# An MLP behind attention on one core: GpSimd rounds the sums of weights, the second bias is loaded first, and the steps of the norm and of the operands stand further apart

## The chip, the cores and the metric

The kernel runs on one core of a Trainium2 chip. A core has TensorE (PE, matrix products, fed by weight loads, PEld), VectorE (DVE), ScalarE (ACT), GpSimd (POOL) and SyncE (SP), which here issues the DMAs. Each engine works through its own instructions in order; they wait for one another by semaphores. The metric is device time in microseconds (us).

## What is computed

One transformer block over 2048 tokens of width 576: modulated layer norm, attention with 32 query heads and one key and value head, and then the part that the change touches, a second modulated norm and an MLP of width 4608.

```python
mod = (_silu(c) @ w_mod).reshape(c.shape[0], 6, 1, -1)
sa, ca, ga, sb, cb, gb = (mod[:, 0], mod[:, 1], mod[:, 2], mod[:, 3], mod[:, 4], mod[:, 5])
h = _layernorm(x, axis=-1) * (1 + ca) + sa
x = x + ga * _A_ref(h, A_wq, A_wk, A_wv, A_wo)          # attention
h = _layernorm(x, axis=-1) * (1 + cb) + sb
x = x + gb * _B_ref(h, B_w1, B_b1, B_w2, B_b2)
# inside _B_ref:
y = _layernorm(x, axis=-1)
h = _gelu(jnp.einsum("bsd,df->bsf", y, w1) + b1)
return jnp.einsum("bsf,fd->bsd", h, w2) + b2
```

## The kernel before

All matrix products are made at close to float32 accuracy from rounded parts. An operand is split in a high part (rounded to `F32R`) and a low part (what the rounding left), and a product is the sum of three: high by high, high by low, low by high. So each operand takes a copy that rounds ("hi") and a subtraction ("lo").

The MLP stage runs over halves of the tokens (1024 each, two blocks of 512) and, within a half, over 18 groups of 256 hidden columns: 36 rounds (`for v in range(NV)`). The product with `w1` of a round covers two blocks of tokens and two halves of the columns, a 2 by 2 by 2 matrix product in blocks, and is made in Strassen's way, with seven products of sums instead of eight. So both operands are needed as sums:

- The weights. `load_w1` brings the raw group into one buffer (`w1r`) a round ahead. `w1_sum(a)` makes the sums numbered 4, 6, 10 and 12 in a scratch tile (`w1s`) on GpSimd and then rounds each with `w1_hi` on ScalarE (L652, into `w1a`); `w1_sum_lo` takes the low part on GpSimd (L655). `w1_a`, `w1_22` and `w1_tails` do the same for the parts that are no sums. This is spread over the round before the one that uses them.
- The tokens. `op_pieces` makes the seven operands (`ops`, and `opt` for the last 64 rows) of a half from the normed tokens `yr`: "+X" rounds piece X on ScalarE (L880), "-X" takes its low part (L882), "=X" forms the difference on VectorE (L873). For the first half they are made at the end of the attention stage and in round 0; for the second half in round 17.

A round goes through its seven products (`product`, L934, into the PSUM tiles `psB`), adds them up on VectorE, runs four `gelu` generators (each alternates between ScalarE and VectorE, and ends with a high part on ScalarE, L953, and a low part on GpSimd, L954), and between them takes the eight tiles of the product with `w2` of the round before (`t_()`, generator `fc2`, L969, into the two tiles `psA`; VectorE adds each into the residual `XT`, L973). The order on each engine is the order of this code. `g_()` steps each gelu once.

Seven calls of `more()` a round place other work. In rounds 1 to 9 they step the second norm of the second half (`ln2_block(2)`, `ln2_block(3)`, four tiles of 128 tokens each): statistics (L138 and the lines after on VectorE, L144 and L145 on GpSimd), apply (L533 on VectorE, L535 and L536 on GpSimd), statistics again, apply again (L547), add the bias `b2` to the residual (L551 on GpSimd), and transpose with PE (L150, evacuated by ScalarE L160 and VectorE L162). A tile takes seven steps, so one a round. The first step also loads the bias `b2g` and scales it on GpSimd (L562 to L564).

PSUM has two `psA` and four `psB` tiles here; a new `psB` must wait until the one that it takes over has been read.

Of the kernel before, what the change touches and what calls it, by code (L numbers as in the profile page):

```python
# [18 lines left out]
KD = 5  # L19
# [13 lines left out]
def block_kernel(ctx: ExitStack, tc, x, wqkv, wo, w1, b1, w2, b2, c, wmod, ident_in, out):  # L33
# [19 lines left out]
    def psB(): return PS["t"].tile([128, 512], F32, name="psB", bufs=PS["b"])  # L53
# [463 lines left out]
    def ln2_tile(tb, t):  # L517

        X = XT[:, NT * tb + t, :]

        def small():
            return (per.tile([128, 2], F32, name="mv2", bufs=2), per.tile([128, 1], F32, name="rs2", bufs=2))

        fine = tb < 2
        mv, rs = small()
        stt = ln_stats1(X)
        if fine:
            yield
# [4 lines left out]
        (po if fine else ve).tensor_scalar(h, X, mv[:, 0:1], rs, op0=ALU.subtract, op1=ALU.mult)  # L533
        e = po if fine else ve
        po.tensor_mul(h, h, BC[:, 1, :])  # L535
# [10 lines left out]
        e = po if fine else ve  # L546
        e.tensor_scalar(h, h, mv[:, 0:1], rs, op0=ALU.subtract, op1=ALU.mult)  # L547
        e.tensor_copy(Z[:, D:], Z[:, 512:D])
        if fine:
            yield  # L550
        po.tensor_tensor(X, X, B2["b"], op=ALU.add)  # L551
        yield
        yr = YR[tb // 2][:, KD * (tb % 2):KD * (tb % 2 + 1)]
        transpose_tile(Z, yr, t, 0, 4, ac)
        yield
        transpose_tile(Z, yr, t, 4, 5, ve)
        yield

    def ln2_block(tb):
        if "b" not in B2:  # L560
            b2g = B2["b"] = px.tile([128, D], F32, name="b2g")
            sy.dma_start(b2g, b2.to_broadcast([128, D]))  # L562
            po.tensor_mul(b2g, b2g, BC[:, 2, :])
            po.tensor_scalar(b2g, b2g, 2.0, None, op0=ALU.mult)  # L564
# [68 lines left out]
    W1 = {}  # L633
# [4 lines left out]
    def w1_rooms():  # L638
        while prep:
            step(prep)  # L640
        W1["a"] = px.tile([128, KD, 2, 128], F32, name="w1r")
        t = px.tile([128, 3, 128], F32, name="w1s")
        W1["s"], W1["d"] = t[:, :2], t[:, 2]

    def w1_raw(f, h):
        return W1["a"][:, 2 * h:2 * h + 2, f, :]

    def load_w1(i):
        sy.dma_start(W1["a"].rearrange("p k f c -> p k (f c)"), w1[i])

    def w1_hi(a, n, src):
        ac.activation(W1["r"][:, a:a + n], src, AF.Copy)  # L652
# [4 lines left out]
    def w1_a(e=po):  # L657
        src = W1["a"][:, :KD - 1, 0, :]
        w1_hi(0, 4, src)
        w1_lo(0, 4, src, e)  # L660

    def w1_22(e=po):
        w1_hi(8, 2, w1_raw(1, 1))
        w1_lo(8, 2, w1_raw(1, 1), e)

    SUMS = {4: "S2", 6: "S3", 10: "S1", 12: "S4"}

    def w1_sum(a, e=po):

        o = W1["s"]  # L670
        def op(x, y, how):
            e.tensor_tensor(o, x, y, op=how)  # L672
        if SUMS[a] == "S3":
            op(w1_raw(0, 0), w1_raw(1, 0), ALU.subtract)
        elif SUMS[a] == "S4":
            op(w1_raw(0, 1), W1["r"][:, 4:6].bitcast(F32), ALU.subtract)
            op(o, W1["r"][:, 21:23].bitcast(F32), ALU.subtract)
        else:
            op(w1_raw(1, 0), w1_raw(1, 1), ALU.add)
            if SUMS[a] == "S2":  # L680
                op(o, w1_raw(0, 0), ALU.subtract)
        w1_hi(a, 2, o)

    def w1_sum_lo(a, e=po):
        w1_lo(a, 2, W1["s"], e)

    def w1_tails(e=po):

        t, d = W1["a"][:, KD - 1], W1["d"]
        ac.activation(W1["r"][:, 14:16], t, AF.Copy)  # L690
# [24 lines left out]
    def first_split():  # L715
        w1_tile()
        w1_rooms()
        load_w1(0)
        for _ in range(3):
            yield  # L720
        w1_sum(4, ve)
        w1_a()
        w1_sum_lo(4, ve)
        yield
        w1_sum(6, ve)
        w1_22()
        w1_sum_lo(6, ve)
        yield
        w1_sum(10, ve)
        w1_sum_lo(10, ve)  # L730
        yield
        w1_sum(12, ve)
        w1_sum_lo(12, ve)
        yield
        w1_tails()
        yield


# [177 lines left out]
    W2 = W2[:2], W2[2:]  # L916
    B2.clear()
    NV = 2 * NG

    def load_w2(v):  # L920
# [61 lines left out]
    def t_():  # L982
        next(f2, None)

    def g_():

        for gen in list(gens):
            if next(gen, 0) == 0:
                gens.remove(gen)

    for v in range(NV):
        nx = v + 1 < NV
        if v == NG - 1:
# [12 lines left out]
        load_w2(v)  # L1006
        ba = psB()
        product(ba, 0, 0)
        ac.activation(U[:, 0], ba, AF.Copy)
# [12 lines left out]
        if nx:  # L1022
            w1_sum(4)
        more("-T2 =T3", "-T1 -t1")
        t_()
        if v == 1:
            t_()
        if nx:
            w1_sum_lo(4)
        product(ba, 2, 2, False, (0, 0))  # L1030
        gens.append(gelu(v, 0, 0, ba))
        g_()
        if nx:
            w1_a()
            w1_sum(6)
        more("+T3 +B21 -B21", "-T4")
        t_()
        if nx:
# [9 lines left out]
        if nx:  # L1048
            w1_sum(10)
        more("-T3 =T4 =T1 +T1", "-B22")  # L1050
        t_()
        if nx:
            w1_sum_lo(10)
        g_()
        product(bc, 8, 12, False, (1, 0))
        ve.tensor_tensor(bc, bc, U[:, 0], op=ALU.add)
        g_()
        gens.append(gelu(v, 1, 0, bc))
        g_()
        if nx:  # L1060
            w1_22()
        more("-T1 +T4 +t0 -t0")
        t_()
        g_()
        t_()
        product(bd, 12, 4, False, (2, 1))
        ve.tensor_tensor(bd, bd, U[:, 0], op=ALU.add)
        g_()
        gens.append(gelu(v, 0, 1, bd))
        g_()  # L1070
        t_()
        if nx:
            w1_sum(12)
            w1_tails()
            w1_sum_lo(12)
# [48 lines left out]
```

## Time and profile before

| | us |
|---|---|
| median of 3 runs | 2455.12 (2451.79 to 2460.95) |
| the profiled execution | 2455.7 |
| its span, first to last instruction | 2453.8 |
| of which to the first product of the MLP stage | 1450.9 |
| from there on | 1002.9 |
| PE busy in the two parts | 1417.9 and 913.5 |

The profile is of one execution. Rows of a timeline give the start, the length, the engine, the line of the code, what is written from what, how many instructions were merged, and in brackets the time that the engine sat idle before, with what ended it. A row of windows gives the stretch and its length, then for each engine the busy time and the number of instructions, the granted PE clock, the DMAs' share and GB/s. A row of waits gives the total, the times and the longest. A row by source line gives the shortest, median and longest in ns.

### The profile page before, as it was taken

What the parts mean: (1) busy time and instruction counts of PE and PEld (TensorE: products, weight loads), DVE (VectorE), ACT (ScalarE), POOL (GpSimd) and SP (SyncE); (2) the same over time, 40 slices, a digit from 0 to 9 for tenths busy, and PEclk for the clock granted to TensorE, in tenths of its full rate; (3) what the DMA queues carried; (4) which work ended last, traced back from release to release, by engine and by line L of the source; (5) the groups of instructions that cost most, each with busy time, mean ns of one, the idle gap of its engine ahead of it and who ended that gap; (6) DMA issues with size and microseconds to landing.
All of it is one profiled execution on the core that took longest, in us unless ns stands there. A gap on an engine that the chain in (4) does not pass through costs nothing. (4 is left out here: it accounts for less than half of the span.)

```text
span 2453.8 us, 43998 instructions
## 1 busy us (share of the span) xinstructions
PE 2331.5 (95%) x16586; PEld 1459.2 (59%) x16586; DVE 1807.8 (74%) x3242; ACT 1741.5 (71%) x3440; POOL 1089.4 (44%) x1226
## 2 busy tenths in 40 slices
PE   8999999999999999999999996988899899999999
PEld 6644444453444544444444355877788688888888
DVE  6589999889999799998899644665555655555555
ACT  5479999979999799998899963444444454444443
POOL 6502233245443245411111026776666666666663
PEclk9999999999999999999999998999999999999999
DMA  6421122112222112100000011111122122212112
GB/s 216 139 65 59 55 62 64 57 48 81 66 62 65 57 43 69 45 19 16 17 22 18 17 35 65 61 61 61 61 77 74 61 99 76 76 61 91 60 63 87
DMA packets 63205, 155.29 MB, mean 63 GB/s; under 512 B 7835, under 2 KB 11547, under 8 KB 62993
## 3 DMA queue, kind: packets, MB, share of 16 engines
q1 hardware_dynamic: 62993, 152.48, 18.9%
q8 instruction: 131, 2.15, 0.4%
q14 instruction: 81, 0.66, 0.1%
HBM read 108.17 MB, written 35.39 MB: 59 GB/s over the span
## 5 line engine op out<-in xcount | busy, mean ns | idle before, releaser
L784 ACT ACTIVATE P<-psB 128x512 f32<-128x512 f32 x2048 | 1050.5, 621 | 4.8 <-PE psB L782 3.4
L804 DVE TENSOR_REDUCE mx<-psM 128x1 f32<-128x512 f32 x1476 | 944.1, 683 | 57.1 <-PE psM L313 34.1
L771 PE MATMUL psC<-P,V 128*32 128x256 f32 (+1 forms) x6056 | 598.5, 467 | 12.9 <-ACT O L604 12.9
L313 PE MATMUL psM<-KS,qst 64*128 64x512 f32 x1722 | 595.4, 432 | 5.3 <-DVE mx L804 5.3
L782 PE MATMUL psB<-qst,KS 64*128 64x512 f32 x2048 | 599.7, 435 | 0.4 <-DMA qst<-ms 0.3
L969 PE MATMUL psA<-w2s,big 128*128 128x288 f32 x2880 | 510.9, 300 | 60.9 <-DVE XT L973 60.5
L969 PEld LDWEIGHTS psA<-w2s,big 128*128 128x128 f32 x2880 | 437.4, 191 | 94.2 <-DVE XT L973 81.7
L934 PE MATMUL psB<-ops,w1a 128*128 128x512 f32 x1512 | 395.8, 401 | 17.1 <-ACT yr L160 10.5
L782 PEld LDWEIGHTS psB<-qst,KS 64*128 64x128 f32 x2048 | 306.3, 184 | 166.6 <-issue 72.5
L313 PEld LDWEIGHTS psM<-KS,qst 64*128 64x128 f32 x1722 | 285.0, 185 | 125.7 <-DVE mx L802 83.6
L934 PEld LDWEIGHTS psB<-ops,w1a 128*128 128x128 f32 x1512 | 275.6, 191 | 70.2 <-ACT yr L160 11.9
L973 DVE TENSOR_TENSOR XT<-psA,XT 128x576 f32<-128x576 f32 x288 | 215.5, 750 | 105.2 <-PE psA L969 103.1
L954 POOL TENSOR_TENSOR big<-gx,big 128x512 fp32r<-128x512 f32 x144 | 187.3, 1300 | 228.2 <-ACT big L953 219.7
L652 ACT ACTIVATE w1a<-w1s 128x256 fp32r<-128x256 f32 x144 | 60.6, 421 | 319.1 <-POOL w1s L672 313.2
L771 PEld LDWEIGHTS psC<-P,V 128*32 128x32 f32 x6056 | 119.6, 108 | 232.5 <-issue 208.9
L953 ACT ACTIVATE big<-gx 128x512 fp32r<-128x512 f32 x144 | 91.0, 632 | 177.6 <-DVE gx L952 167.2
L795 ACT ACTIVATE xc<-psB 128x512 f32<-128x512 f32 x246 | 147.5, 600 | 91.1 <-PE psM L313 80.3
L355 POOL CAST ms<-mf 16x128 fp32r<-16x128 f32 x32 | 9.0, 280 | 408.1 <-ACT mf L354 408.1
L949 DVE SCALAR_TENSOR_TENSOR gs<-psB,gx 128x512 f32<-128x512 f32 x144 | 99.4, 690 | 100.1 <-ACT psB L947 99.6
L969 PE MATMUL psA<-w1a,big 128*128 128x288 f32 x576 | 170.7, 296 | 0.0
L802 DVE CUSTOM_DVE_ANT_0 xc<-psM,xc 128x512 f32<-128x512 f32 x246 | 167.4, 680 | 0.0
L952 DVE SCALAR_TENSOR_TENSOR gx<-psB,gx 128x512 f32<-128x512 f32 x144 | 98.9, 687 | 89.7 <-ACT psB L950 89.4
(168 smaller groups left out, 2638.4 us busy)
## 6 DMA issues: line engine op xcount, KB each, us to landing
w2s<-w2scr SPq DMA_DIRECT2D x54, 576.0 KB
w1r<-in_w SPq DMA_DIRECT2D x36, 640.0 KB
w2scr<-w2p SPq DMA_DIRECT2D x36, 576.0 KB
qst<-qscr SPq DMA_DIRECT2D x192, 72.0 KB
w2o<-in_w SPq DMA_DIRECT2D x36, 288.0 KB
w1a<-w2scr SPq DMA_DIRECT2D x18, 576.0 KB
qscr<-qs SPq DMA_DIRECT2D x16, 504.0 KB
big<-os SPq DMA_DIRECT2D x112, 72.0 KB
```

The source lines that it names most:

```text
L313: pe.matmul(o, QST[n][64 * g:64 * g + 64, p, 128 * qt:128 * (qt + 1)], KS[64 * g:64 * g + 64, 512 * kb:512 * (kb + 1)], start=True, stop=True)
L771: pe.matmul(PVt[n][32 * j:32 * (j + 1), cs], V[:, kc, :], t[:, j, cs], start=(kc == 0 and h0 == 0), stop=(kc == 15), skip_group_check=True)
L782: pe.matmul(t, KS[64 * g:64 * g + 64, 128 * kc:128 * (kc + 1)], QST[n][64 * g:64 * g + 64, i, :], start=True, stop=True)
L784: ac.activation(P[n, kc][:, 2 * i + g, :], t, AF.Exp, scale=SCALE)
L795: ac.activation(XC[-1], t, AF.Relu)
L802: ve.tensor_tensor_reduce(c, t, c, 1.0, -3.0e38, ALU.add, ALU.max, o)
L804: ve.tensor_reduce(o, t, axis=AX.X, op=ALU.max)
L934: pe.matmul(o, x, y, start=(first and i == 0), stop=(i == len(terms) - 1), skip_group_check=True)
L949: ve.scalar_tensor_tensor(s, p, 1.0 / GA3, h, op0=ALU.add, op1=ALU.mult)
L954: po.tensor_tensor(GT[:, 2 * u + 1], h, GT[:, 2 * u].bitcast(F32), op=ALU.subtract)
L969: pe.matmul(p[:, nn, :288], x, y, start=(q == 0), stop=(q == len(terms) - 1))
L973: ve.tensor_tensor(Xv, p[:, :, :288], Xv, op=ALU.add)
```

## The change

Five edits in one:

1. `w1_sum` rounds its result on GpSimd (a cast, `tensor_copy`) where GpSimd made the sum, and takes the low part directly behind it. The difference in `w1_tails` is rounded on GpSimd too. 176 instructions go from ScalarE to GpSimd. The other parts keep ScalarE, with the high and the low part set at different places in the round.
2. The bias of the second half is loaded ahead of the weights at the start of the MLP stage, and scaled before round 0.
3. A tile of the norm of the second half has eight steps. Steps that end in `"T"` have a transpose next, and such a step is taken only at the third and the fourth `more` of a round.
4. Operands for the first half: `+T4`, `-T4`, `+B22` and `-B22` go into round 0, `-t1` and `-T1` ahead of it.
5. Operands for the second half: the pieces stand at other places of round 17, and `-T1 -B22 -t1` in round 18.

```diff
@@ ln2_tile
         po.tensor_tensor(h, h, BC[:, 0, :], op=ALU.add)
         yield
+        if not fine:
+            yield
         mv, rs = small()
...
         po.tensor_tensor(X, X, B2["b"], op=ALU.add)
-        yield
+        yield None if fine else "T"
         yr = YR[tb // 2][:, KD * (tb % 2):KD * (tb % 2 + 1)]
         transpose_tile(Z, yr, t, 0, 4, ac)
-        yield
+        yield None if fine else "T"
         transpose_tile(Z, yr, t, 4, 5, ve)
         yield
+    def load_b2():
+        b2g = px.tile([128, D], F32, name="b2g")
+        sy.dma_start(b2g, b2.to_broadcast([128, D]))
+        return b2g
+    def b2_scaled(b2g):
+        po.tensor_mul(b2g, b2g, BC[:, 2, :])
+        po.tensor_scalar(b2g, b2g, 2.0, None, op0=ALU.mult)
+        return b2g
@@ the weights
-    def w1_hi(a, n, src):
-        ac.activation(W1["r"][:, a:a + n], src, AF.Copy)
+    def w1_hi(a, n, src, e=ac):
+        o = W1["r"][:, a:a + n]
+        if e is ac:
+            ac.activation(o, src, AF.Copy)
+        else:
+            e.tensor_copy(o, src)
...
-        w1_hi(a, 2, o)
-    def w1_sum_lo(a, e=po):
-        w1_lo(a, 2, W1["s"], e)
+        w1_hi(a, 2, o, e if e is po else ac)
+        w1_lo(a, 2, o, e)
...
         e.tensor_tensor(d, t[:, 0], t[:, 1], op=ALU.subtract)
-        ac.activation(W1["r"][:, 16], d, AF.Copy)
+        e.tensor_copy(W1["r"][:, 16], d)
@@ the start of the MLP stage
-    form("=T4 =T1 +T1 +t1 +T4 +B22")
+    form("+t1 =T4 =T1 +T1 -t1 -T1")
     open_ps("3", 4)
     w1_rooms()
+    B2["b"] = load_b2()
     load_w1(1)
...
+    b2_scaled(B2["b"])
+    mark = [None]
@@ a round
-        def more(w="", first=""):
-            if 0 < v < NG - 1:
-                step(fill)
-            elif v == NG - 1:
-                form(w)
-            elif v == 0:
-                form(first)
+        def more(half="", first="", room=False):
+            if v in (0, NG - 1, NG):
+                form(first if v == 0 else half if v == NG - 1 else "-T1 -B22 -t1" if first == "+T4" else "")
+            elif v < NG and fill and (room or mark[0] != "T"):
+                mark[0] = next(fill[0], "end")
+                if mark[0] == "end":
+                    fill.popleft()
...
-        more("+B11 -B11")
+        more("+B11", "+T4")
...
-        more("+T2")
+        more("-B11 +T2", "-T4")
...
-        if nx:
-            w1_sum(4)
-        more("-T2 =T3", "-T1 -t1")
+        wt(w1_sum, 4)
+        more("-T2 =T3", "+B22", True)
...
-            w1_a()
-            w1_sum(6)
-        more("+T3 +B21 -B21", "-T4")
+        wt(w1_part, 0, False)
+        more("+T3 +B21", "-B22", True)
         t_()
-        if nx:
-            w1_sum_lo(6)
         g_()
+        wt(w1_sum, 6)
+        wt(w1_part, 0, True)
...
-        more("-T3 =T4 =T1 +T1", "-B22")
+        more("-T3 -B21 =T4")
...
-        more("-T1 +T4 +t0 -t0")
+        more("=T1 +T4 +t0")
...
-        more("-T4 +B22 -B22 +t1 -t1")
+        more("-T4 -t0 +T1 +B22 +t1")
```

`wt(f, ...)` calls `f` in all rounds but the last; `w1_part(a, lo)` makes the high or the low part of what `w1_a` and `w1_22` made.

How the engines' rows change, at three places. First SyncE at the start of the MLP stage, with the DMAs that it issues for rounds 0 and 1: `w1r` the raw weights, `w2s` and `w1a` the weights of the second product, `b2g` the bias. Before:

```order
L626 DMA big<-os 18x2x512 x4
L649 DMA w1r<-in_w 128x1280
L922 DMA w2s<-w2scr 128x1152 x2
L649 DMA w1r<-in_w 128x1280
L922 DMA w2s<-w2scr 128x1152
L922 DMA w1a<-w2scr 128x1152
L562 DMA b2g<-in_b 128x576
```

and in the change:

```order
L634 DMA big<-os 18x2x512 x4
L562 DMA b2g<-in_b 128x576
L657 DMA w1r<-in_w 128x1280
L932 DMA w2s<-w2scr 128x1152 x2
L657 DMA w1r<-in_w 128x1280
```

The bias moved ahead of five loads. Second, ScalarE in the first part of a plain round (round 19): `u` is the copy of the first product, `gx`, `psB<-gs` and `big` the steps of a gelu, `w1a<-w1s` the rounding of a sum. Before:

```order
L1009 ACTIVATE u<-psB 128x512
L950 ACTIVATE psB<-gs 128x512
L953 ACTIVATE big<-gx 128x512
L652 ACTIVATE w1a<-w1s 128x256
L946 ACTIVATE gx<-psB,b1t 128x512
L947 ACTIVATE psB<-psB,b1t 128x512
L652 ACTIVATE w1a<-w1r 128x512
L652 ACTIVATE w1a<-w1s 128x256
L950 ACTIVATE psB<-gs 128x512
L953 ACTIVATE big<-gx 128x512
```

and in the change:

```order
L1027 ACTIVATE u<-psB 128x512
L960 ACTIVATE psB<-gs 128x512
L963 ACTIVATE big<-gx 128x512
L956 ACTIVATE gx<-psB,b1t 128x512
L957 ACTIVATE psB<-psB,b1t 128x512
L662 ACTIVATE w1a<-w1r 128x512
L960 ACTIVATE psB<-gs 128x512
L963 ACTIVATE big<-gx 128x512
```

The two roundings of sums are gone from between the gelu steps. Third, VectorE in round 17, from the step of the fifth `more` on: `ops<-yr,ops` is a low part, `yr<-yr` a difference, `XT<-psA,XT` the evacuation of a tile of the second product. Before:

```order
L882 TENSOR_TENSOR ops<-yr,ops 128x1024
L873 TENSOR_TENSOR yr<-yr 128x1024 x2
L973 TENSOR_TENSOR XT<-psA,XT 128x576
L949 SCALAR_TENSOR_TENSOR gs<-psB,gx 128x512
L1056 TENSOR_TENSOR psB<-psB,u 128x512
L952 SCALAR_TENSOR_TENSOR gx<-psB,gx 128x512
L882 TENSOR_TENSOR ops<-yr,ops 128x1024
L973 TENSOR_TENSOR XT<-psA,XT 128x576
```

and in the change:

```order
L892 TENSOR_TENSOR ops<-yr,ops 128x1024
L883 TENSOR_TENSOR yr<-yr 128x1024
L983 TENSOR_TENSOR XT<-psA,XT 128x576
L959 SCALAR_TENSOR_TENSOR gs<-psB,gx 128x512
L1066 TENSOR_TENSOR psB<-psB,u 128x512
L962 SCALAR_TENSOR_TENSOR gx<-psB,gx 128x512
L883 TENSOR_TENSOR yr<-yr 128x1024
L983 TENSOR_TENSOR XT<-psA,XT 128x576
```

One of the two differences moved behind an evacuation, and the low part after it left this place.

More of the change, by code (lines that the diff above doesn't have):

```diff
@@ L532, in ln2_tile @@
         h = Z[:, :D]
-        (po if fine else ve).tensor_scalar(h, X, mv[:, 0:1], rs, op0=ALU.subtract, op1=ALU.mult)
         e = po if fine else ve
+        e.tensor_scalar(h, X, mv[:, 0:1], rs, op0=ALU.subtract, op1=ALU.mult)
         po.tensor_mul(h, h, BC[:, 1, :])
@@ L545, in ln2_tile @@
             yield
-        e = po if fine else ve
         e.tensor_scalar(h, h, mv[:, 0:1], rs, op0=ALU.subtract, op1=ALU.mult)
@@ L551, in ln2_tile @@
         po.tensor_tensor(X, X, B2["b"], op=ALU.add)
-        yield
+        yield None if fine else "T"
         yr = YR[tb // 2][:, KD * (tb % 2):KD * (tb % 2 + 1)]
         transpose_tile(Z, yr, t, 0, 4, ac)
-        yield
+        yield None if fine else "T"
         transpose_tile(Z, yr, t, 4, 5, ve)
         yield
+    def load_b2():
[6 more added lines that the diff above has]
+        return b2g
     def ln2_block(tb):
         if "b" not in B2:
[L561 to L564, printed above, removed]
+            B2["b"] = b2_scaled(load_b2())
         if tb % 2 == 0:
@@ L649, in load_w1, with w1_part @@
         sy.dma_start(W1["a"].rearrange("p k f c -> p k (f c)"), w1[i])
-    def w1_hi(a, n, src):
-        ac.activation(W1["r"][:, a:a + n], src, AF.Copy)
+    def w1_hi(a, n, src, e=ac):
[4 more added lines that the diff above has]
+            e.tensor_copy(o, src)
     def w1_lo(a, n, src, e):
         e.tensor_tensor(W1["r"][:, 17 + a:17 + a + n], src, W1["r"][:, a:a + n].bitcast(F32), op=ALU.subtract)
[L657 to L664, printed above, removed]
+    def w1_part(a, lo, e=po):
+        n, src = (4, W1["a"][:, :KD - 1, 0, :]) if a == 0 else (2, w1_raw(1, 1))
+        if lo:
+            w1_lo(a, n, src, e)
+        else:
+            w1_hi(a, n, src)
     SUMS = {4: "S2", 6: "S3", 10: "S1", 12: "S4"}
@@ L681, in w1_sum, with w1_tails @@
                 op(o, w1_raw(0, 0), ALU.subtract)
-        w1_hi(a, 2, o)
-    def w1_sum_lo(a, e=po):
-        w1_lo(a, 2, W1["s"], e)
-    def w1_tails(e=po):
+        w1_hi(a, 2, o, e if e is po else ac)
+        w1_lo(a, 2, o, e)
+    def w1_tails(lo, e=po):
         t, d = W1["a"][:, KD - 1], W1["d"]
-        ac.activation(W1["r"][:, 14:16], t, AF.Copy)
+        if not lo:
+            w1_hi(14, 2, t)
+            return
         e.tensor_tensor(d, t[:, 0], t[:, 1], op=ALU.subtract)
-        ac.activation(W1["r"][:, 16], d, AF.Copy)
+        e.tensor_copy(W1["r"][:, 16], d)
         for o, i in ((slice(14, 16), t), (16, d)):
@@ L721, in first_split @@
         w1_sum(4, ve)
-        w1_a()
-        w1_sum_lo(4, ve)
+        w1_part(0, False)
         yield
+        w1_part(0, True)
         w1_sum(6, ve)
-        w1_22()
-        w1_sum_lo(6, ve)
         yield
+        w1_part(8, False)
         w1_sum(10, ve)
-        w1_sum_lo(10, ve)
+        w1_tails(False)
         yield
+        w1_part(8, True)
         w1_sum(12, ve)
-        w1_sum_lo(12, ve)
         yield
-        w1_tails()
+        w1_tails(True)
         yield
@@ L916, in block_kernel @@
     W2 = W2[:2], W2[2:]
-    B2.clear()
     NV = 2 * NG
@@ L996, in block_kernel, with wt @@
             form = op_pieces(YR[1], po)
-        def more(w="", first=""):
-            if 0 < v < NG - 1:
-                step(fill)
-            elif v == NG - 1:
-                form(w)
-            elif v == 0:
-                form(first)
+        def more(half="", first="", room=False):
[5 more added lines that the diff above has]
+                    fill.popleft()
+        def wt(f, *a):
+            if nx:
+                f(*a)
         load_w2(v)
@@ L1027, in block_kernel @@
             t_()
-        if nx:
-            w1_sum_lo(4)
         product(ba, 2, 2, False, (0, 0))
@@ L1032, in block_kernel @@
         g_()
-        if nx:
-            w1_a()
-            w1_sum(6)
-        more("+T3 +B21 -B21", "-T4")
-        t_()
-        if nx:
-            w1_sum_lo(6)
-        g_()
+        wt(w1_part, 0, False)
+        more("+T3 +B21", "-B22", True)
+        t_()
+        g_()
+        wt(w1_sum, 6)
+        wt(w1_part, 0, True)
         bd = psB()
@@ L1047, in block_kernel @@
         g_()
-        if nx:
-            w1_sum(10)
-        more("-T3 =T4 =T1 +T1", "-B22")
-        t_()
-        if nx:
-            w1_sum_lo(10)
+        more("-T3 -B21 =T4")
+        t_()
         g_()
+        wt(w1_sum, 10)
         product(bc, 8, 12, False, (1, 0))
@@ L1059, in block_kernel @@
         g_()
-        if nx:
-            w1_22()
-        more("-T1 +T4 +t0 -t0")
+        wt(w1_part, 8, False)
+        more("=T1 +T4 +t0")
         t_()
@@ L1065, in block_kernel @@
         t_()
+        wt(w1_part, 8, True)
         product(bd, 12, 4, False, (2, 1))
@@ L1070, in block_kernel @@
         g_()
+        wt(w1_tails, False)
         t_()
[L1072 to L1075, printed above, removed]
-        more("-T4 +B22 -B22 +t1 -t1")
+        wt(w1_sum, 12)
+        wt(w1_tails, True)
+        more("-T4 -t0 +T1 +B22 +t1")
         drain(f2)
```

## The prediction

> **What bounds the kernel now.** First the page: its busy shares, its slices, and the granted clock.
>
> ```profile
> span 2453.8 us, 43998 instructions
> PE 2331.5 (95%) x16586; PEld 1459.2 (59%) x16586; DVE 1807.8 (74%) x3242; ACT 1741.5 (71%) x3440; POOL 1089.4 (44%) x1226
> PE   8999999999999999999999996988899899999999
> PEclk9999999999999999999999998999999999999999
> ```
>
> PE is busy nearly everywhere, so time can only come from the places where it isn't: one slice at about 1470 to 1530 us, the slices after it, and one near 1960. All lie in the MLP stage, which the change touches. I cut that stage into its 36 rounds. A round begins with a group of 12 products on PE; the edges below are those starts (round 0, round 1, rounds 2 to 9, 10 to 16, 17 and 18, 19 to 34, and the products and eight tiles of round 35).
>
> ```profile
> core 0: us, PE busy (x) PEld busy (x) DVE busy (x) ACT busy (x) POOL busy (x), PEclk, DMA share, GB/s
> 1450.94:1469.83 18.89, 13.94 (x50) 10.33 (x51) 11.62 (x15) 9.61 (x16) 8.02 (x9) 0.91 0.26 98
> 1469.83:1514.55 44.72, 27.22 (x152) 23.95 (x151) 19.93 (x34) 17.63 (x34) 27.66 (x31) 0.81 0.13 49
> 1514.55:1754.20 239.65, 211.13 (x1206) 185.95 (x1205) 135.97 (x238) 103.15 (x205) 170.82 (x203) 0.96 0.17 62
> 1754.20:1934.09 179.89, 174.00 (x1025) 154.17 (x1023) 98.84 (x148) 88.51 (x176) 112.06 (x133) 1.00 0.20 72
> 1934.09:1999.69 65.60, 52.26 (x295) 46.12 (x293) 41.50 (x51) 32.87 (x60) 44.97 (x42) 0.92 0.23 84
> 1999.69:2411.75 412.06, 397.51 (x2339) 352.55 (x2337) 225.62 (x337) 202.35 (x401) 256.02 (x304) 1.00 0.21 74
> 2411.75:2436.20 24.45, 24.45 (x149) 22.16 (x148) 14.33 (x22) 12.00 (x23) 9.88 (x11) 1.00 0.15 49
> ```
>
> A round costs 412.06/16 = 25.75 us where nothing extra happens, 239.65/8 = 29.96 where the norm of the second half of the tokens runs beside it, 44.72 in round 1, and 65.60 for rounds 17 and 18 together. Round 35 prepares no weights, and takes 24.45 with PE busy throughout. **So 24.45 is PE's own time for a round; all above it is waiting.** Where it waits, in order of time:
>
> ```profile
> 1454.87 0.73 POOL L672 TENSOR_TENSOR w1s<-w1r 128x256 f32<-128x256 f32 x1 [19.71 <-DMA w1r<-in_w]
> 1457.71 1.67 PE L934 MATMUL psB<-ops,w1a 128*128 128x512 f32 x6 [2.29 <-ACT u L1009]
> 1466.75 2.50 PE L934 MATMUL psB<-ops,w1a 128*128 128x512 f32 x5 [2.38 <-DVE ops L882]
> ...
> 1480.71 0.51 SPq L562 DMA_DIRECT2D b2g<-in_b  x1
> 1487.03 1.40 POOL L563 TENSOR_TENSOR b2g<-b2g,BC 128x576 f32<-128x576 f32 x1 [6.50 <-DMA b2g<-in_b]
> 1488.51 1.67 POOL L564 TENSOR_SCALAR b2g<-b2g 128x576 f32<-128x576 f32 x1
> 1491.07 1.51 DVE L533 TENSOR_SCALAR Z<-XT,mv,rs 128x576 f32<-128x576 f32 x1 [10.63 <-POOL rs L145]
> 1497.30 3.25 PE L969 MATMUL psA<-w2s,big 128*128 128x288 f32 x12 [15.99 <-DVE XT L973]
> ...
> 1512.85 0.27 PE L150 MATMUL psB<-ident,Z 128*128 128x128 f32 x1
> 1533.34 0.66 PE L150 MATMUL psB<-ident,Z 128*128 128x128 f32 x4 [2.41 <-DVE Z L547]
> 1661.56 2.93 PE L934 MATMUL psB<-ops,w1a 128*128 128x512 f32 x6 [2.63 <-ACT yr L160]
> ...
> 1922.95 0.42 ACT L652 ACTIVATE w1a<-w1s 128x256 fp32r<-128x256 f32 x1 [2.10 <-POOL w1s L672]
> 1927.40 0.42 ACT L652 ACTIVATE w1a<-w1s 128x256 fp32r<-128x256 f32 x1 [0.96 <-POOL w1s L672]
> 1930.99 0.69 DVE L949 SCALAR_TENSOR_TENSOR gs<-psB,gx 128x512 f32<-128x512 f32 x1 [1.22 <-ACT psB L947]
> 1932.40 0.40 PE L969 MATMUL psA<-w2s,big 128*128 128x288 f32 x1 [0.72 <-DVE XT L973]
> ...
> 1948.65 1.85 PE L969 MATMUL psA<-w2s,big 128*128 128x288 f32 x12 [1.69 <-DVE XT L973]
> 1958.47 3.94 DVE L873 TENSOR_TENSOR yr<-yr 128x1024 f32<-128x1024 f32 x2
> 1963.14 3.25 PE L969 MATMUL psA<-w2s,big 128*128 128x288 f32 x12 [9.16 <-DVE XT L973]
> ```
>
> Each row names in brackets how long the engine sat idle and for whom. Round 1: the bias load (L562) is issued behind that round's weights, GpSimd stops for it, the statistics (L145) stand behind it on GpSimd, VectorE holds for them, and PE for VectorE. The tiles after long stalls also run slowly, 12 matmuls in 3.25 against 1.85 us.
>
> **The change, part by part.**
>
> *Rounded sums go to GpSimd (176 casts).* Four ScalarE copies of 128x256 and one of 128x128 in a round become GpSimd casts. The trace has that cast in two other sizes:
>
> ```profile
> L707 POOL CAST w2p<-w2o x36: 652/657/670, 276.1 to 993.7; 128x576 fp32r<-128x576 f32 x36
> L355 POOL CAST ms<-mf x32: 279/280/285, 132.7 to 1394.4; 16x128 fp32r<-16x128 f32 x32
> ACT w1a L652 <- POOL w1s L672: 313.2, 138, 15.9
> POOL big L954 <- ACT big L953: 219.7, 135, 6.6
> ```
>
> A straight line through the two (128 and 576 columns) gives 0.39 us for 256 columns; the bounds are 0.28 and 0.66. GpSimd gains 4 x 0.39 + 0.28 = 1.84 us a round on the 16.0 it has (256.02/16), 17.8 of 24.7: it stays below PE, which is its cover. ScalarE loses its 138 waits of 313.2 us in total. This is worth PE time in every round, by this chain in round 16: ScalarE stands 2.10 and then 0.96 us for GpSimd's sums, the tanh behind it is late, then the next gelu, so VectorE's L949 waits 1.22 and the evacuation of a PSUM tile queued behind L949 comes 0.72 too late for PE. Taking over 2 us out of the front of that chain removes the 0.72 and the smaller lags. In round 35, where these copies are absent, that stall is absent too. Bounds for a plain round: 24.45 and 25.75. I take 24.7, near the row of round 35, since only GpSimd's share is heavier than there. Added waits: each cast waits for PE to have read the old weights; behind it on GpSimd stand the low parts of gelu (L954), which PE needs in the next round, and the reload of the raw weights (SP, L649), which waits for the last low part and took 1454.87 - 1450.82 = 4.05 us from its issue at 1450.82 to its reader.
>
> ```profile
> 1450.82 0.35 SPq L649 DMA_DIRECT2D w1r<-in_w  x1
> ```
>
> By the Trainium skill (GPSIMD Engine Reference, section 4.1, Engine selection), elementwise work belongs on VectorE, since GpSimd is about twice as slow on two inputs and near line rate on one. The trace agrees: 0.657 us for the one-input cast of 576 columns, 1.40 for the two-input L563. By its two-input price GpSimd (0.73 for 256 columns in the row of 1454.87) would stand at 16.0 + 5 x 0.73 = 19.7 us a round, still under 24.7, and the sum would not change.
>
> Rounds 19 to 34: 16 x 24.7 = 395.2, **saving 16.9** (bounds 0 and 20.9).
>
> *Bias first; first operands in another order (rounds 0 and 1).* The bias load now leads SP's queue at 1450.82, before the weights; every later load moves back by one issue, 0.5 us. GpSimd scales it (1.40 + 1.67) before its first sum, where it was idle for the weights until 1454.87 anyway: with the bias there by about 1453 (it has fewer bytes ahead of it than the weights, which took 4.05) its start slips some 1.5 us and from there its chain no longer waits for ScalarE's copies. In round 0 ScalarE copies the first product sooner, as `+T4 +B22` no longer stand ahead of it, and `-T1` is ahead of its reader: I drop the 2.29 and 2.38 stalls, 18.89 to 14.2. In round 1 the 15.99 goes, with 3.25 - 1.85 = 1.4 of slow matmuls: 44.72 to 27.3. What is late next is GpSimd itself: it must end round 0's weights before the first norm's statistics, and VectorE's norm step waits for those with PE's evacuations behind it. The bounds of that are 0 and 9.6 us (the load's 6.50 and the scaling's 3.07, if GpSimd comes as late as it did); I take 5, half. Together 63.61 to 46.5, **saving 17.1** (8, if the stalls of round 0 stay too, to 22).
>
> *Norm steps set further apart.* Eight tiles take 8 steps each where they took 7, and transposes only at two places in a round, after the third and fourth product, where PSUM tiles are free. Counting the steps through the loop, they fill rounds 1 to 13 (before: 1 to 9). PE's own work, one group of four transposes (0.66) and one single (0.27), stays: about 0.93 a tile. The 2.41 wait for Z should mostly go, a pause now lying before it, and the 2.63 for ScalarE's evacuation too. I leave 1.07 a tile of stall (bounds 0 and 5.04, both old ones). Rounds 2 to 16: 15 x 24.7 + 8 x 2.0 = 386.5 against 419.54, **saving 33.0** (bounds 1.5 and 45). Of this 15 is the plain gain again. GpSimd's norm work, 170.82/8 - 16.0 = 5.35 us a tile, is now spread: two tiles in three rounds, 17.8 + 3.6 = 21.4 a round, 23.2 in the fullest.
>
> *Operands of the second half (rounds 17, 18).* The three VectorE pieces in a row that end in the 9.16 stall (a low part, then L873 twice for 3.94) are split over three places, and one low part each goes to round 18. Round 17 keeps `-T2 =T3` together, which had the 1.69. I leave 5 us over two plain rounds, 54.4 against 65.60, **saving 11.2** (bounds 5 and 16.7). That L873 took 1.97 each there beside busy GpSimd, and 1.24 each (2.48) alone:
>
> ```profile
> 1451.20 2.48 DVE L873 TENSOR_TENSOR yr<-yr 128x1024 f32<-128x1024 f32 x2
> ```
>
> The Trainium skill (SBUF — State Buffer, Who interferes with whom) calls this an exclusive lock between the two engines. By it the extra casts could lengthen these pieces too, by at most a cast each, 8 x 0.39 = 3 us, which would make the saving 8.
>
> At the end of the attention stage ScalarE loses one copy of 128x128; PE's last products there hide it, and I count 0 (a fraction of a us if not). The sum: 16.9 + 17.1 + 33.0 + 11.2 = 78.2. The profiled execution took 2455.7 (1.9 outside its span), 0.6 above the median of the runs; **2455.7 - 78.2 = 2377.5**, about 2377.
>
> **Rivals.**
> - *Plain rounds don't shrink*: PE's 0.72 is set by VectorE's order, not by ScalarE. For: the named releaser is VectorE. Against: round 35. Then 31 rounds are 1.0 longer: 2377 + 32 = 2409.
> - *Norm rounds stay starved*: GpSimd at 23.2 us plus a reload that it must wait for (4.05, partly covered by a gelu part) exceeds 24.7, and its late statistics hold VectorE. For: VectorE's wait of 10.63. Against: the average of 21.4. At 1.7 in 12 rounds: 2397.
> - *Bias not early in effect*: GpSimd gets it no sooner than the weights and round 1 keeps two thirds of its stall: 2388.
> - *Slower: GpSimd becomes the ring.* If its waits for ScalarE's gelu copies stay (219.7/36, 6 us a round), the reload leaves 2.3 idle (4.05 less one gelu part and a tail), and a cast costs 0.73 like the two-input L672, a round is 16.0 + 3.7 + 6 + 2.3 = 28.0; from 25.75 on it decides. 31 rounds x 2.25 = 70 more than before, less 28 for rounds 0, 1, 17 and 18: about 2497. Against: those waits exist because ScalarE is late.
>
> **How the numbers follow.** Forecast 0.60 (2355 to 2398), plain rounds unchanged 0.18, norm rounds starved 0.13, bias late 0.04, slower 0.03, the rest 0.02. The range takes in the forecast, its better bounds and the first three rivals: 2352 to 2416. Half a per cent is 12 us, about what a measurement of this kernel can tell; faster than 2443 in all cases but the ring and part of the rest: 0.94, same 0.03, slower 0.03.
>
> **What would show it.** Right: plain rounds at 24.5 to 24.9 with no 0.72 wait, ScalarE waiting no more for w1s; the stall at round 1 under 6 us; casts near 0.39; rounds 17 and 18 under 57. Wrong: plain rounds still 25.7; GpSimd waiting for reloads, VectorE for rs by several us in rounds 2 to 13; transposes still waiting over 2 us.

## The result, and the profile after

The changed kernel takes **2369.22 us** (median of 4 runs, 2367.2 to 2371.97), the kernel before 2456.64 beside it: ratio **0.9645, 95% interval 0.9624 to 0.9667**. The forecast was 2377, range 2352 to 2416.

The page of the profiled execution, its first lines and two of its slices:

```profile
span 2365.4 us, 44038 instructions
PE 2310.6 (98%) x16586; PEld 1456.1 (62%) x16586; DVE 1822.6 (77%) x3242; ACT 1693.2 (72%) x3264; POOL 1157.7 (49%) x1402
PE   8999999999999999999999999999999999999999
PEclk9999999999999999999999999999999999999999
```

The dip near 1500 us and the one near 1960 are gone from PE's slices. GpSimd is busy for 68 us more. The windows, cut at the starts of the same rounds (0 and 1, 2 to 16, 17 and 18, 19 to 34, and the last):

```profile
core 0: us, PE busy (x) PEld busy (x) DVE busy (x) ACT busy (x) POOL busy (x), PEclk, DMA share, GB/s
1452.19:1499.62 47.43, 40.65 (x197) 33.94 (x197) 31.97 (x47) 23.92 (x40) 39.30 (x48) 0.93 0.26 85
1499.62:1876.76 377.14, 372.44 (x2233) 336.51 (x2232) 246.45 (x386) 173.13 (x310) 313.99 (x412) 1.00 0.20 74
1876.76:1933.50 56.74, 50.89 (x295) 45.83 (x293) 40.08 (x50) 28.85 (x48) 47.17 (x52) 0.94 0.27 96
1933.50:2323.57 390.07, 390.07 (x2338) 353.57 (x2337) 229.17 (x337) 181.26 (x323) 287.08 (x385) 1.00 0.21 78
2323.57:2348.10 24.53, 24.53 (x149) 22.24 (x148) 14.31 (x21) 10.43 (x19) 9.66 (x13) 1.00 0.15 49
```

Rounds 19 to 34 are now PE's own time: busy 390.07 of 390.07 us, 24.38 a round. Round 35 alone had shown 24.45 before. The span went from 2453.8 to 2365.4. Of these 88.4 us, 88.2 come from the following places, the rest from behind round 34:

| rounds | before | after | saved | forecast |
|---|---|---|---|---|
| 0 and 1 | 63.61 | 47.43 | 16.2 | 17.1 |
| 2 to 16 | 419.54 | 377.14 | 42.4 | 33.0 |
| 17 and 18 | 65.60 | 56.74 | 8.9 | 11.2 |
| 19 to 34 | 412.06 | 390.07 | 22.0 | 16.9 |
| the start of round 0 | 1450.94 | 1452.19 | -1.2 | 0 |

What is left of waiting, in rows of the timeline (in brackets the idle time before, and what ended it):

```profile
1452.07 0.36 SPq L562 DMA_DIRECT2D b2g<-in_b  x1
1457.25 1.43 POOL L566 TENSOR_TENSOR b2g<-b2g,BC 128x576 f32<-128x576 f32 x1 [27.99 <-DMA b2g<-in_b]
1461.28 0.82 POOL L683 TENSOR_TENSOR w1s<-w1r 128x256 f32<-128x256 f32 x1
1467.56 2.60 PE L944 MATMUL psB<-ops,w1a 128*128 128x512 f32 x10 [2.13 <-POOL w1a L667]
1472.24 1.79 PE L944 MATMUL psB<-ops,w1a 128*128 128x512 f32 x6 [2.07 <-DVE gx L962]
1479.98 1.52 DVE L534 TENSOR_SCALAR Z<-XT,mv,rs 128x576 f32<-128x576 f32 x1 [3.16 <-POOL rs L145]
1482.82 2.41 PE L979 MATMUL psA<-w2s,big 128*128 128x288 f32 x12 [2.33 <-DVE XT L983]
...
1582.19 0.66 PE L150 MATMUL psB<-ident,Z 128*128 128x128 f32 x4 [2.36 <-DVE Z L548]
...
1895.18 2.34 POOL L892 TENSOR_TENSOR ops<-yr,ops 128x1024 fp32r<-128x1024 f32 x1
1897.55 1.73 DVE L883 TENSOR_TENSOR yr<-yr 128x1024 f32<-128x1024 f32 x1 [4.72 <-POOL ops L892]
1898.26 1.27 POOL L664 CAST w1a<-w1s 128x256 fp32r<-128x256 f32 x1
1900.00 3.25 PE L979 MATMUL psA<-w2s,big 128*128 128x288 f32 x12 [5.33 <-DVE XT L983]
```

Three places. In rounds 0 and 1 GpSimd begins its first sum only at 1461.28, behind the bias, and PE waits 2.13 us for the weights that it makes, 2.07 for a step of a gelu, and 2.33 behind a VectorE step that waited 3.16 for GpSimd's statistics. In rounds 2 to 16 the transposes of three tiles wait for Z, 2.36, 1.18 and 1.16 us. And in round 17 VectorE's difference `=T4` waits for GpSimd's low part `-B21`, whose source it overwrites.

### The profile page after: what moved, and what is told of

Same layout as the page of the kernel before. It is cut to its first block, busy times and chain, and to the rows that moved or that the text cites. A ratio compares the mean times of both kernels' runs of the same rounds, so it can differ in the third digit from the quotient of the medians.

```text
span 2365.4 us, 44038 instructions
## 1 busy us (share of the span) xinstructions
PE 2310.6 (98%) x16586; PEld 1456.1 (62%) x16586; DVE 1822.6 (77%) x3242; ACT 1693.2 (72%) x3264; POOL 1157.7 (49%) x1402
## 4 chain that ended last, share of the span: by engine, by line
PE 89%; DVE 3%; ACT 3%; POOL 3%; issue 1%; DMA 1%; SPq 0%; POOLq 0%; DVEq 0%; ACTq 0%
PE psC L781 21%; PE psA L979 19%; PE psB L944 17%; PE psB L792 11%; PE psM L313 10%; PE psB L802 4%; PE psB L593 2%; PE psB L242 2%; ACT P L794 2%; DVE mx L814 1%; PE psB L150 1%; PE psA L313 1%; PE psB L197 1%; ACT O L612 1%; DMA bigw<-in_wmod 0%
## 5 line engine op out<-in xcount | busy, mean ns | idle before, releaser
L814 DVE TENSOR_REDUCE mx<-psM 128x1 f32<-128x512 f32 x1476 | 944.3, 683 | 57.5 <-PE psM L313 33.0
L979 PE MATMUL psA<-w2s,big 128*128 128x288 f32 x2880 | 498.1, 297 | 8.5 <-DVE XT L983 8.5
L944 PE MATMUL psB<-ops,w1a 128*128 128x512 f32 x1512 | 390.8, 398 | 4.6 <-POOL w1a L667 2.1
L956 ACT ACTIVATE gx<-psB,b1t 128x512 f32<-128x512 f32 x144 | 97.3, 675 | 105.8 <-PE psB L944 97.3
L960 ACT ACTIVATE psB<-gs 128x512 f32<-128x512 f32 x144 | 86.5, 601 | 94.3 <-DVE gs L959 94.3
```

The costliest lines, as they stand in the source:

```text
L814: ve.tensor_reduce(o, t, axis=AX.X, op=ALU.max)
L944: pe.matmul(o, x, y, start=(first and i == 0), stop=(i == len(terms) - 1), skip_group_check=True)
L979: pe.matmul(p[:, nn, :288], x, y, start=(q == 0), stop=(q == len(terms) - 1))
```

## The experiments

The start of round 0 lies between 1449.0 and 1457.7 us in these runs, with an attention stage that differs only at its end, in the first weights and operands. So parts are compared by the length of their rounds, and totals by the ratio. "Before" and "changed" say which kernel was edited.

### 1. Changed, with the sums rounded on ScalarE again

```diff
-        w1_hi(a, 2, o, e if e is po else ac)
+        w1_hi(a, 2, o)
...
-        e.tensor_copy(W1["r"][:, 16], d)
+        ac.activation(W1["r"][:, 16], d, AF.Copy)
```

> The changed kernel with one thing undone: the sums of weights (and the difference in the tails) are rounded on ScalarE again, at the same places in the round; all the rest stays as changed. Theory (ScalarE, waiting in its queue for GpSimd's sums, is what makes a plain round longer than PE's own 24.4 us): rounds 19 to 34 go back from 390 to about 412 us, the 0.7 us wait of PE for VectorE's evacuation is back in each, and the whole takes about 2369 + 22 + 15 x 1.2 = 2409. Rival (the new places of the high and low parts did it, not the engine): rounds 19 to 34 stay at 390 and the whole at 2369.

2383.83 us, ratio 0.9712 (0.9698 to 0.9727). The windows of rounds 2 to 16, 17 and 18, and 19 to 34:

```profile
1502.73:1889.18 386.45, 375.48 (x2232) 338.06 (x2231) 236.51 (x386) 197.77 (x385) 285.45 (x337) 0.99 0.20 72
1889.18:1950.72 61.54, 51.65 (x294) 45.77 (x293) 40.03 (x50) 32.11 (x58) 43.55 (x42) 0.94 0.24 89
1950.72:2340.80 390.08, 390.08 (x2338) 353.55 (x2337) 225.85 (x337) 208.19 (x403) 256.55 (x305) 1.00 0.21 78
```

The plain rounds stay at 24.38, with every rounding back on ScalarE. The theory as I had put it falls for them. Elsewhere the engine does count: rounds 2 to 16 take 386.5 us for 377.1 to 382.4 in two profiles of the changed kernel (experiment 9 has the second), rounds 17 and 18 61.5 for 56.7 and 57.6, so the rival's total of 2369 isn't reached either.

ScalarE still waits in the plain rounds: first its waits for the sums in rounds 19 to 34 of the kernel before, then in this one (total, times, longest).

```profile
ACT w1a L652 <- POOL w1s L672: 130.8, 64, 4.0
```

```profile
ACT w1a L662 <- POOL w1s L683: 71.6, 34, 3.0
```

The waits that remain, some two a round, are those for the sums 4 and 12. Their 71.6 us in those 16 rounds cost PE nothing. The waits for the sums 6 and 10 are gone, as ScalarE's rows in one round show, from sum 4 (2131.39) over sum 6 (2134.34) on:

```profile
2131.39 0.42 ACT L662 ACTIVATE w1a<-w1s 128x256 fp32r<-128x256 f32 x1 [2.96 <-POOL w1s L683]
2131.71 0.67 ACT L956 ACTIVATE gx<-psB,b1t 128x512 f32<-128x512 f32 x1
2132.28 0.65 ACT L957 ACTIVATE psB<-psB,b1t 128x512 f32<-128x512 f32 x1
2132.86 0.63 ACT L662 ACTIVATE w1a<-w1r 128x512 fp32r<-128x512 f32 x1
2133.80 0.60 ACT L960 ACTIVATE psB<-gs 128x512 f32<-128x512 f32 x1 [0.32 <-DVE gs L959]
2134.34 0.40 ACT L662 ACTIVATE w1a<-w1s 128x256 fp32r<-128x256 f32 x1
```

The rounding of sum 6 now stands behind the tanh (L960), and waits for nothing. In the kernel before it stood ahead of the tanh and held it for 2.10 us. But the order on GpSimd changed as well. Before, sum 6 stood behind a low part of 512 columns, and now it stands ahead of it (the rows of round 16 before, then of the round above):

```profile
1920.93 1.29 POOL L655 TENSOR_TENSOR w1a<-w1r,w1a 128x512 fp32r<-128x512 f32 x1 [0.93 <-ACT w1a L652]
1922.18 0.74 POOL L672 TENSOR_TENSOR w1s<-w1r 128x256 f32<-128x256 f32 x1
```

```profile
2132.70 0.74 POOL L683 TENSOR_TENSOR w1s<-w1r 128x256 f32<-128x256 f32 x1
2135.51 1.30 POOL L667 TENSOR_TENSOR w1a<-w1r,w1a 128x512 fp32r<-128x512 f32 x1
```

Sum 6 ends at 2133.44, ahead of the tanh at 2133.80. So the new places were enough in plain rounds; how much of that is ScalarE's order and how much GpSimd's was not tried.

### 2. Before, with the casts alone

```diff
-        w1_hi(a, 2, o)
+        if e is po:
+            po.tensor_copy(W1["r"][:, a:a + 2], o)
+        else:
+            w1_hi(a, 2, o)
...
-        ac.activation(W1["r"][:, 16], d, AF.Copy)
+        e.tensor_copy(W1["r"][:, 16], d)
```

> The kernel before with one thing changed: the sums of weights and the difference in the tails are rounded on GpSimd, at their old places. Theory: rounds 19 to 34 fall from 412 to about 390, rounds 10 to 16 from 180 to 171, the norm's rounds 2 to 9 by some 8, while the 16 us stall of round 1 and the 9 us stall of round 17 stay: about 2455 - 22 - 9 - 8 = 2416. Rival (the engine of the rounding is not what costs): 2455.

2386.33 us, ratio 0.9722 (0.9706 to 0.9738): 30 us better than expected. Its windows, rounds 0 and 1 first:

```profile
1454.00:1516.83 62.83, 40.53 (x201) 33.95 (x202) 31.50 (x48) 24.86 (x43) 39.29 (x48) 0.86 0.17 64
1516.83:1895.81 378.98, 373.13 (x2227) 334.49 (x2226) 238.86 (x385) 171.60 (x307) 312.66 (x412) 1.00 0.20 74
1895.81:1952.61 56.80, 50.88 (x294) 46.00 (x293) 40.96 (x50) 30.25 (x51) 49.46 (x53) 0.94 0.27 97
1952.61:2342.69 390.08, 390.08 (x2338) 353.60 (x2337) 228.89 (x336) 180.09 (x322) 286.39 (x385) 1.00 0.21 78
```

The engine alone is enough too in the plain rounds. What I had not expected are the two lines between: the norm's rounds with the old seven steps, 378.98 us, and rounds 17 and 18 with the old order of the operands, 56.80, are as fast as in the changed kernel (377.14 and 56.74). Only rounds 0 and 1 keep their stall.

### 3. Before, with the bias first alone

```diff
+    B2["b"] = load_b2()
     load_w1(1)
...
+    b2_scaled(B2["b"])
     for v in range(NV):
```

> The kernel before with one thing changed: the second bias is loaded ahead of the weights at the start of the MLP stage and scaled on GpSimd before round 0. Theory (the late bias load is the cause of the stall of round 1): rounds 0 and 1 fall from 63.6 to about 50, the whole to about 2442. Rival (GpSimd is late with round 0's weights anyway and VectorE waits for the statistics just as long): rounds 0 and 1 above 58, the whole above 2449.

2444.17 us, ratio 0.9961 (0.9946 to 0.9976). Rounds 0 and 1 take 1451.82 to 1507.90, 56.1 us, between the theory's 50 and the rival's 58. PE's stall in round 1:

```profile
1490.28 3.25 PE L976 MATMUL psA<-w2s,big 128*128 128x288 f32 x12 [6.33 <-DVE XT L980]
```

15.99 became 6.33. Here too it is followed by twelve matmuls at 3.25 us, so that part of the loss stays. The late load with its scaling was the main cause. What is left goes with the norm's seven steps: experiment 4, which has these steps and the casts, shows 6.85 us at this place, the changed kernel with eight steps 2.33.

### 4. Changed, with the norm's seven steps back

```diff
-        if not fine:
-            yield
         mv, rs = small()
...
-        yield None if fine else "T"
+        yield
...
-        yield None if fine else "T"
+        yield
```

> The changed kernel with one thing undone: the norm of the second half takes seven steps a tile again, transposes at the sixth and seventh place of a round. Theory (their place matters: PE waits 2.4 us a tile for Z, or 2.6 for the evacuation): rounds 2 to 16 go from 377 to about 377 + 8 x 3 = 401, the whole to 2393 (2385 to 2404). Rival (the waits were ScalarE's lateness, gone with the casts): rounds 2 to 16 at most 385, the whole at most 2377.

2381.29 us, ratio 0.9704 (0.969 to 0.9719). Rounds 2 to 16:

```profile
1504.90:1888.70 383.80, 373.69 (x2227) 334.20 (x2226) 240.10 (x385) 172.06 (x307) 313.56 (x412) 1.00 0.20 73
```

These 383.8 us are the rival's 385, not 401; the total is 4 us above the rival's 2377 and below the theory's 2385. Against 377.1 to 382.4 in two profiles of the changed kernel (experiment 9) the wider spacing is worth 1 to 7 us there. In rounds 0 and 1 it is worth 3.5 to 4.6 (52.0 against 47.4 and 48.5), since PE's stall in round 1 is 6.85 us without it.

### 5 and 6. Before, with two of the sums on GpSimd, and with the others

```diff
-        w1_hi(a, 2, o)
+        if e is po and a in (6, 10):
+            po.tensor_copy(W1["r"][:, a:a + 2], o)
+        else:
+            w1_hi(a, 2, o)
```

Experiment 6 has (4, 12) for (6, 10), and the difference of the tails is rounded on GpSimd as well.

> The kernel before with one thing changed: only the sums 6 and 10 are rounded on GpSimd, at their old places. Refined theory (what costs a plain round are the two roundings that stand ahead of a tanh in ScalarE's queue, those of the sums 6 and 10, where ScalarE stood 2.1 and 1.0 us for GpSimd; the changed places put them behind the tanh, the casts take them away, and either is enough): rounds 19 to 34 at 390 to 394 us, the whole at about 2390. Rival (any of the five copies that leaves ScalarE helps by its share): rounds 19 to 34 about 402, the whole near 2420.

> The counterpart: the kernel before with only the sums 4 and 12 and the difference of the tails rounded on GpSimd, at their old places. Refined theory: ScalarE's longest waits go (3.1 and 1.8 us a round), but they stood ahead of nothing that PE waits for, so rounds 19 to 34 stay at 408 to 412 and the whole at 2440 or more. Rival (share of the copies): rounds 19 to 34 about 399, the whole near 2412.

Experiment 5: 2402.98 us, ratio 0.9796 (0.9781 to 0.9812). Experiment 6: 2424.26, ratio 0.9881 (0.9866 to 0.9897). Rounds 19 to 34 of each:

```profile
1968.82:2358.90 390.08, 390.08 (x2339) 353.56 (x2338) 228.98 (x337) 193.78 (x371) 269.23 (x337) 1.00 0.21 78
```

```profile
1981.29:2381.30 400.01, 393.99 (x2339) 353.49 (x2338) 227.61 (x337) 189.89 (x353) 273.31 (x352) 1.00 0.21 76
```

The sums 6 and 10, the two on the chain that the prediction read, bring the plain rounds to 24.38 by themselves, though ScalarE still waits for the others. The sums 4 and 12 bring half (400.0): the refined theory, by which they bring nothing, missed, and the rival's 399, a share for each copy, was met here, though its 402 for experiment 5 was not. So the copies don't simply add up. The waits for 4 and 12 cost PE nothing by themselves (experiments 1 and 5), but they cost some 12 us while those for 6 and 10 stand. Why is not shown. In the norm's rounds all five copies count: experiment 5 has 393.4 us in rounds 2 to 16, the full set of casts 379.0.

### 7. Changed, with each cast done twice

```diff
             e.tensor_copy(o, src)
+            e.tensor_copy(o, src)
...
         e.tensor_copy(W1["r"][:, 16], d)
+        e.tensor_copy(W1["r"][:, 16], d)
```

> The changed kernel with each of the 176 casts done twice, which writes the same values again and adds some 1.9 us a round to GpSimd. Theory (GpSimd has room, PE is the bound of a plain round): rounds 19 to 34 stay at 390, the whole within 6 us of 2369, what is added being in rounds 0 to 13. Rival (GpSimd is close to being the ring): rounds 19 to 34 at 400 or more, the whole above 2385.

2396.27 us, ratio 0.977 (0.975 to 0.9789). Rounds 2 to 16 and 19 to 34, and VectorE in round 5:

```profile
1507.89:1907.40 399.51, 379.24 (x2233) 341.51 (x2231) 247.29 (x386) 174.51 (x310) 341.20 (x487) 0.98 0.19 70
1967.04:2357.11 390.07, 390.07 (x2338) 353.57 (x2337) 228.97 (x337) 181.47 (x324) 316.01 (x465) 1.00 0.21 78
```

```profile
1593.30 1.51 DVE L548 TENSOR_SCALAR Z<-Z,mv,rs 128x576 f32<-128x576 f32 x1 [3.69 <-POOL rs L145]
```

GpSimd carries 316.0/16 = 19.8 us in a plain round of 24.38 and it costs nothing there. The norm's rounds lose 17 to 22 us: VectorE waits for statistics that stand behind the casts (at the place of this row 3.69 us, 0.66 in the changed kernel), PE for Z. So GpSimd has room in plain rounds and next to none in the norm's. The total is above the rival's 2385, but not for its reason: it was wrong about the ring, and my 6 us were wrong about the norm.

### 8. Changed, with `-B21` at the fourth place of round 17

```diff
-        more("+T3 +B21", "-B22", True)
+        more("+T3 +B21 -B21", "-B22", True)
...
-        more("-T3 -B21 =T4")
+        more("-T3 =T4")
```

> The changed kernel with one piece of the operands moved: the low part -B21, on GpSimd, stands at the fourth place of round 17 as before, not at the fifth. In the changed kernel VectorE's difference =T4 overwrites what -B21 reads, waits 4.7 us for it behind three other steps of GpSimd, and PE waits 5.3. Theory: that wait goes, rounds 17 and 18 fall from 56.7 to about 51, the whole to about 2363. Rival (VectorE's five pieces set it): rounds 17 and 18 above 55.

2366.3 us, ratio 0.9645 (0.9616 to 0.9675): by the total alone undecided. Rounds 17 and 18:

```profile
1881.67:1934.72 53.05, 49.95 (x294) 44.01 (x293) 40.70 (x50) 29.01 (x48) 48.42 (x52) 1.00 0.30 103
```

That is 53.05 us against 56.74, not quite the 51 expected. The 5.33 us wait is no longer there; waits of 1.26, 0.94 and 0.74 are.

### 9 to 12. Three further edits of the changed kernel

Experiment 9 is the changed kernel again. Experiment 10 loads the bias in round 0, behind the weights of the first two rounds, and scales it in round 1:

```diff
-    B2["b"] = load_b2()
     load_w1(1)
...
-    b2_scaled(B2["b"])
...
         load_w2(v)
+        if v == 0:
+            B2["b"] = load_b2()
...
         if not fine:
+            if (tb, t) == (2, 0):
+                b2_scaled(B2["b"])
             yield
```

Experiment 11 adds an empty step ahead of the transposes:

```diff
         po.tensor_tensor(X, X, B2["b"], op=ALU.add)
+        if not fine:
+            yield
         yield None if fine else "T"
```

Experiment 12 has both, and `-B21` of experiment 8.

> The changed kernel once more, unaltered, on the same chip and in the same call as the three that follow, to compare them with: rounds 0 and 1 at 47.4 us, 2 to 16 at 377 to 381, 17 and 18 at 56.7, 19 to 34 at 390, the whole at about 2369.

> The changed kernel with the bias loaded behind the weights of rounds 0 and 1, and scaled on GpSimd in round 1, at the third place, instead of before round 0. In the changed kernel the bias takes 5.2 us to land, GpSimd starts its first sum at 1461.3, 6.4 us later than in the kernel before, and PE waits 2.1 and 2.3 us on GpSimd's account in rounds 0 and 1. Theory (the early scaling costs that): rounds 0 and 1 fall from 47.4 to about 43. Rival (the chain of gelu steps sets rounds 0 and 1, or the scaling costs the same in round 1): 46 to 49.

> The changed kernel with one more empty step of a norm tile, between the second apply and the transposes, so that these never stand at neighbouring places. In the changed kernel they do in rounds 5, 10 and 13, and PE waits for Z there, 1.2 to 2.4 us each. Theory: the three waits go and rounds 2 to 16 fall from 377 to 381 to about 371 (15 x 24.38 and 8 x 0.7 of transposes). Rival (GpSimd is full in the norm's rounds and the wait moves elsewhere): 376 or more.

> The changed kernel with -B21 at the fourth place, the bias loaded behind the weights, and the empty step before the transposes, all three together. If each does what its theory says, rounds 0 and 1 at 43, 2 to 16 at 371, 17 and 18 at 53, and the whole 4 + 8 + 4 = 16 us below the changed kernel, at about 2354. Rival: what one frees is waited for elsewhere, and the whole is above 2362.

| | us | ratio to before | 0 and 1 | 2 to 16 | 17 and 18 |
|---|---|---|---|---|---|
| 9, changed again | 2371.8 | 0.9662 (0.9643 to 0.9681) | 48.5 | 382.4 | 57.6 |
| 10, bias behind | 2368.87 | 0.9653 (0.9637 to 0.9669) | 46.8 | 375.5 | 57.5 |
| 11, empty step | 2362.54 | 0.9622 (0.9608 to 0.9635) | 47.4 | 370.1 | 57.5 |
| 12, all three | 2356.26 | 0.96 (0.9586 to 0.9614) | 46.7 | 370.1 | 53.5 |

The repeat in experiment 9 has 382.4 us in rounds 2 to 16, above the 381 expected: its three waits for Z are 2.36 us each. So a difference of 5 us in these rounds can lie between two executions of one kernel.

In experiment 12:

```profile
1495.74:1865.81 370.07, 370.07 (x2232) 335.21 (x2231) 244.92 (x387) 174.04 (x311) 313.75 (x413) 1.00 0.21 75
1865.81:1919.34 53.53, 49.94 (x294) 43.98 (x293) 41.24 (x50) 29.18 (x48) 49.64 (x53) 1.00 0.29 102
1919.34:2309.42 390.08, 390.08 (x2339) 353.57 (x2337) 229.21 (x337) 181.35 (x324) 287.54 (x385) 1.00 0.21 78
```

The empty step does what its theory said: rounds 2 to 16 are PE's own time, with no wait left and 0.54 us of transposes a tile (24.92 and 24.38 us in turn). The same instructions run, and GpSimd's 313.75 us fit. The bias behind the weights brings only 0.6 to 1.7 us in rounds 0 and 1, in the rival's range. PE's wait for GpSimd's first weights falls from 2.13 to 0.46 us, but behind it stand 2.28 us for a gelu step and 3.46 behind the norm's VectorE step, for 2.07 and 2.33 in the changed kernel (0.77 and 3.45 in its repeat). Which of the rival's two reasons it is, the gelu chain or the scaling set in round 1, is not shown. In sum experiment 12 is below both kernels, its interval clear of that of the changed kernel beside it.

## Why the prediction was right, and where not

- **A plain round waits on ScalarE, which waits for GpSimd's sums.** Right in the mechanism and in the two waits read (2.10 and 0.96 us, for the sums 6 and 10), by experiment 5. The size was off: 24.7 a round was taken, and it is 24.38, so the term of rounds 19 to 34 came out at 22.0 for 16.9. Round 35's row gave the number; I added 0.25 for GpSimd's load, which experiment 7 shows to cost nothing.
- **The casts as the cause.** Only half right. The prediction put the gain on the copies that leave ScalarE; experiment 1 gives the same plain rounds with none leaving, because the change also set the sums and their roundings at other places. Either is enough in plain rounds. Taken alone the casts bring 67 us (experiment 2); the rest of the change without them, 70 (experiment 1); both together 87.
- **GpSimd's price.** Estimated 0.39 us a cast, measured 0.397 (shortest, median and longest in ns):

```profile
L664 POOL CAST w1a<-w1s x140: 396/397/1273, 1463.0 to 2325.5; 128x256 fp32r<-128x256 f32 x140
```

- **The norm's steps set apart save their waits.** This step failed as a cause. The sum of 33.0 for rounds 2 to 16 came out at 42.4, but the waits of 2.41 and 2.63 us are gone in experiments 2 and 4 too, where the old seven steps stand beside the casts: they went with the casts. The spacing itself is worth 1 to 7 there. The prediction credited 18 us of the 33.0 to the steps and 15 to the plain gain; that these rounds came out no further from its sum is luck, for the casts brought most of those 18. The stall that I left in, 1.07 us a tile, was about right on the average (0.9 and 1.5 in the two profiles, from 377.1 and 382.4 against the 370.1 of experiment 11) and wrong in kind: it falls on the three tiles whose apply and transposes are neighbours. And 0.93 us a tile for PE's own transposes is 0.54.
- **Rounds 17 and 18.** The 9.16 us stall fell to 5.33, so 11.2 became 8.9. The step that was off is "I leave 5 us over two plain rounds", made by the 1.69 us of `-T2 =T3`: two plain rounds are 48.8, so 8.0 were left. Most of it is the new wait of `=T4` for `-B21`, which the change put next to it and which the prediction did not look for. Experiment 2, in the old order, has 5.92 us of stall and the same 56.8 us, so on top of the casts the new order brought nothing.
- **Rounds 0 and 1.** 17.1 was forecast and 16.2 measured, by terms that miss both ways. The bias went ahead of six loads (`w2s` stands for two of them), not five. The bias took 5.2 us from its issue (1452.07) to GpSimd's step, where I had it there within about 2; GpSimd's first sum began at 1461.28, where I had it 1.5 us behind 1454.87. Of PE's waits, 2.13 for GpSimd's weights and 2.33 for the norm stand where I took 5 in all; the 2.07 for a gelu step, 1.38 in the kernel before, I had not counted.
- **The rivals.** Plain rounds unchanged and GpSimd as the ring are refuted by the rows above. Of the rival on the bias the premise came true, for GpSimd got it at 1457.25, later than it had got its weights before (1454.87), and the effect did not: round 1 keeps 2.33 of the 15.99 us. "Norm rounds starved" did not come true here, but experiment 7 shows how near it is: 1.9 us more a round on GpSimd bring it about.
- **VectorE and GpSimd beside each other.** Longer pieces were priced at 3 us on rounds 17 and 18. The cast's longest, 1.27 us for 0.40, is there (1898.26), beside VectorE's difference `=T4`, which took 1.73. Whether this cost PE anything was not tried.

## What to carry to other kernels

An instruction that nobody waits for soon can still be the bound, if it waits at the head of an in-order queue for a slower engine and a step of the critical chain stands behind it: set both at other places or move it to the engine that made its input, and test both, for either may do. The total of a wait (130.8 us in 16 rounds here) says little; the question is what is queued behind it, and the 71.6 us of it that stayed in experiment 1 cost nothing. A stretch of the same program without the suspected work, such as the last round here, gives the floor in advance, and should be believed.

## What the runs showed of the hardware that was not expected

PE was held without a gap for 16 rounds: 390.07 us busy in 390.07, at a granted clock of 1.00; ten further profiles of this study have 390.07 or 390.08 for these rounds. A 128x576 load, broadcast from one row and issued first, took 5.2 us from its issue to its reader, where the 640 KB behind it had taken 4.05 in the kernel before. The two casts of 1.27 us for 0.40 (1898.26 and 1911.38) are the only ones of the 140 above 0.65, and both lie beside a VectorE step of 1024 columns.
